# The second layer of a token-block MLP as seven half-size products instead of eight, on one Trainium2 core

## The chip, the cores and the metric

The kernel runs on one core of a Trainium2 (trn2) chip. A core has TensorE (PE in the profile; PEld is its weight load), VectorE (DVE), ScalarE (ACT), GpSimd (POOL) and SyncE (SP), and 16 DMA engines. The metric is the device time in microseconds (us). Kernels are compared by the runs of the same rounds: a ratio is worked out from these runs, and is not quite the ratio of the medians quoted beside it. TensorE was granted 0.994 to 1.0 of its clock. "Faster" needs 2%. The span in a profile (first to last instruction) is about 1.8 us shorter than the time.

## The reference, cut to what matters

Linear attention, then a gated MLP over 4608 tokens:

```python
# q, k, v: (8, 8, 576, 64); phi(x) = elu(x) + 1
kv  = einsum('bhsd,bhse->bhde', phi(k), v);  z = phi(k).sum(axis=2)
x   = einsum('bhsd,bhde->bhse', phi(q), kv) / (einsum('bhsd,bhd->bhs', phi(q), z) + 1e-6)
x   = x.transpose(...).reshape(4608, 512)
g   = x @ w_gate                               # 512 -> 1536
out = (g * sigmoid(g) * (x @ w_val)) @ w_out   # 1536 -> 512
```

The kernel works in f16 with f32 sums. It handles the MLP in nine groups of 512 tokens. In a group the **first layer** is 12 blocks (`fb`) of 8 matmuls of 512 columns, and the **second layer** multiplies the hidden block h (1536 x 512 tokens) by `w_out`. While a group runs, VectorE and ScalarE prepare the attention of later batches. `pV`, `pG` and `pX` are the eight banks of PSUM, the memory that TensorE writes its sums to; an *eviction* copies a bank to SBUF, the core's working memory.

## The kernel before

The second layer of one group takes four token tiles of 128, twelve matmuls of 512 columns each, and one eviction per tile:

```python
def l2(g, t, f0=0, f1=FB):                       # FB = 12
    pso[(g, t)] = (pV[0], pG[0], pV[1], pG[1])[t]
    for fb in range(f0, f1):
        nc.tensor.matmul(out=pso[(g, t)][:, :], lhsT=hT[g % 2][:, fb, P * t:P * t + P],
                         rhs=wo[:, fb, :], start=(fb == 0), stop=(fb == FB - 1))
```

The tile that ends the kernel is split into two halves of 256 columns (`l2_last`), so that its outputs can leave sooner. In the main loop, ahead of the fourth tile, two small pieces of TensorE work for later groups are made: `mm2` (the next group's x) and, right behind it, `joint` (k'v of the batch after):

```python
for t in range(4):
    if t == 3 and b1 < NG:
        mm2(b1, pV[2], "AVAV")      # next x: 16 small products for most groups, four evictions
        if b2 < B:
            joint(b2)               # next kv: small products, diagonals, R copies
    ...
    l2(g, t)
    for f in w[t] + pre[t]:         # exps and phi of later batches
        f()
    l2_out(g, t, A if t in (1, 3) else V)
```

`phi` of a batch costs VectorE a minimum and two `scalar_tensor_tensor` (max and add in one) per half:

```python
def phi(src, e, dst, b, lp):
    s = slice(2 * lp, 2 * lp + 2)
    nc.vector.tensor_scalar(out=e[:, s, :], in0=e[:, s, :], scalar1=1.0, scalar2=None, op0=ALU.min)
    for l in range(2 * lp, 2 * lp + 2):
        nc.vector.scalar_tensor_tensor(
            out=dst[b % 2][:, :, D * l:D * l + D],
            in0=src[b % 2][:, l, :].rearrange("p (j d) -> p j d", d=D), scalar=0.0,
            in1=e[:, l, :].rearrange("p (j d) -> p j d", d=D), op0=ALU.max, op1=ALU.add)
```

## Time and profile before

The time was 320.99 us (median of 3 runs, 320.7 to 321.11). The page's busy times, and its chain of the work that ended last, read:

```profile
span 319.2 us, 5573 instructions
...
PE 311.8 (98%) x2191; PEld 148.5 (47%) x2191; DVE 211.3 (66%) x393; ACT 171.3 (54%) x246; POOL 31.9 (10%) x47
...
PE 89%; DMA 4%; DVE 2%; POOL 2%; ACT 2%; issue 1%; SPq 0%; POOLq 0%; ACTq 0%
...
```

TensorE is busy for 98% and is 89% of the chain. Busy alone proves little, since the matmul ends are modelled; the starts say more. These are TensorE's lines of the timeline in one second layer and at the kernel's end (start, length, engine, line, operation, out<-in, shapes, count):

```profile
240.53 2.75 PE L303 MATMUL pV<-wo,hT 128*128 128x512 f16 x12
243.12 2.75 PE L303 MATMUL pG<-wo,hT 128*128 128x512 f16 x12
245.71 2.75 PE L303 MATMUL pV<-wo,hT 128*128 128x512 f16 x12
...
311.79 1.47 PE L324 MATMUL pG<-wo,hT 128*128 128x256 f16 x12
313.10 1.47 PE L324 MATMUL pX<-wo,hT 128*128 128x256 f16 x12
...
```

Twelve matmuls of 512 columns start 2.59 us apart, 0.216 us each; twelve of 256 columns 1.31 us apart, 0.109 us each. So matmuls of half the size cost half, although each has its own weight load. One whole group in the middle (window of group 4; columns: window, length, then busy us and instruction counts of each engine, clock, DMA share, GB/s):

```profile
154.35:186.96 32.61, 32.61 (x234) 15.21 (x233) 26.12 (x49) 19.55 (x29) 1.48 (x2) 1.00 0.56 105
```

A group takes 32.61 us: 20.94 for the first layer with one more product of 512 columns (the denominators of a later batch), and 11.67 for the second with `mm2` and `joint`. VectorE is busy for 26.1 us of it and ScalarE for 19.6.

At the end of the kernel, the last evictions and output DMAs follow the last matmul:

```profile
313.76 0.38 ACT L335 ACTIVATE osb<-pG 64x256 f32<-64x256 f32 x1 [3.75 <-DVE osb L332]
313.91 1.67 SPq L338 DMA_DIRECT2D out_dram<-osb  x2
...
314.67 0.42 DVE L332 TENSOR_SCALAR osb<-pX 64x256 f32<-64x256 f32 x1 [0.95 <-PE pX L324]
315.68 0.38 ACT L335 ACTIVATE osb<-pX 64x256 f32<-64x256 f32 x1 [1.55 <-DMA out_dram<-osb]
316.09 0.48 ACTq L338 DMA_DIRECT2D out_dram<-osb  x1
```

From the end of the last matmul (314.58) to the end of the span are 4.62 us. ScalarE's last eviction waits for a DMA that still reads its buffer.

### The profile page before, as it was taken

To read this page: it belongs to the slowest core of one execution; us is meant where nothing else is said; L and a number is where in the kernel's file an instruction comes from. 1 tells how busy PE (TensorE), PEld (TensorE's weight loads), DVE (VectorE), ACT (ScalarE), POOL (GpSimd) and SP (SyncE) were. 2 spreads that over 40 slices of the span, in tenths; PEclk is the share of its full clock that TensorE was granted. 3 is DMA by queue.
4 is the path that set the end of the run, shared out by engine and by line. 5 is a ranking of instruction groups with operands and counts; after the bars stand their busy time and mean duration, and the time that the engine had idled before them with its cause. 6 is when DMAs were issued, how large, how long until landed. Compare 5 with 4: busy or idle time off the path is not lost.

```text
span 319.2 us, 5573 instructions
## 1 busy us (share of the span) xinstructions
PE 311.8 (98%) x2191; PEld 148.5 (47%) x2191; DVE 211.3 (66%) x393; ACT 171.3 (54%) x246; POOL 31.9 (10%) x47
## 2 busy tenths in 40 slices
PE   8999999999999999999999999999999999999994
PEld 6644453444444454445444454445444444444443
DVE  3747749878978877887888787877883344134411
ACT  3869969748563765467536754585431333133310
POOL 8535310010020001000010000000000000000000
PEclk9999999999999999999999999999999999999999
DMA  7999999994579147924792430233022400140014
GB/s 101 194 200 200 204 207 208 260 210 85 118 140 166 33 93 139 154 46 90 142 149 50 87 74 0 49 71 89 2 49 59 101 0 0 35 99 0 2 35 97
DMA packets 40986, 32.21 MB, mean 101 GB/s; under 512 B 16256, under 2 KB 36480, under 8 KB 40960
## 3 DMA queue, kind: packets, MB, share of 16 engines
q0 software_dynamic: 20640, 18.88, 38.0%
q1 hardware_dynamic: 20160, 12.85, 18.4%
q8 instruction: 17, 0.28, 0.4%
q10 hardware_dynamic: 160, 0.13, 0.2%
q14 instruction: 9, 0.07, 0.1%
HBM read 37.75 MB, written 9.44 MB: 148 GB/s over the span
## 4 chain that ended last, share of the span: by engine, by line
PE 89%; DMA 4%; DVE 2%; POOL 2%; ACT 2%; issue 1%; SPq 0%; POOLq 0%; ACTq 0%
PE pV L282 28%; PE pG L282 27%; PE pV L303 14%; PE pG L303 13%; DMA wv<-in_moe_w_val_dram 3%; PE pX L282 2%; PE pX L254 1%; DVE osb L313 1%; DMA out_dram<-osb 1%; PE pV L172 1%; DVE xT L435 1%; ACT rr L432 1%; ACT rr L429 1%; POOL k L99 0%; POOL v L99 0%
## 5 line engine op out<-in xcount | busy, mean ns | idle before, releaser
L288 DVE SCALAR_TENSOR_TENSOR hT<-pV,sil 128x512 f16<-128x512 f32 x105 | 72.2, 691 | 57.0 <-PE pV L282 53.2
L282 PE MATMUL pV<-xT,wv 128*128 128x512 f16 x420 | 108.1, 379 | 0.3 <-DMA wv<-in_moe_w_val_dram 0.3
L282 PE MATMUL pG<-xT,wg 128*128 128x512 f16 x408 | 105.1, 379 | 0.7 <-DVE osb L313 0.6
L287 ACT ACTIVATE sil<-pG 128x512 f16<-128x512 f32 x102 | 60.6, 597 | 78.4 <-PE pG L282 51.2
L282 PEld LDWEIGHTS <-wv 128*128 128x128 f16 x432 | 42.2, 98 | 51.6 <-DMA wv<-in_moe_w_val_dram 1.1
L282 PEld LDWEIGHTS <-wg 128*128 128x128 f16 x432 | 41.8, 98 | 51.0 <-issue 1.5
L303 PEld LDWEIGHTS <-hT 128*128 128x128 f16 x420 | 39.8, 98 | 47.6 <-issue 1.2
L303 PE MATMUL pV<-wo,hT 128*128 128x512 f16 x216 | 50.2, 379 | 0.0
L303 PE MATMUL pG<-wo,hT 128*128 128x512 f16 x204 | 47.6, 380 | 0.0
L313 DVE TENSOR_SCALAR osb<-pV 128x512 f32<-128x512 f32 x18 | 12.4, 690 | 25.3 <-PE pV L303 25.3
L311 ACT ACTIVATE osb<-pG 128x512 f32<-128x512 f32 x15 | 8.8, 589 | 19.9 <-PE pG L303 19.8
L127 DVE SCALAR_TENSOR_TENSOR kp<-k,ek 128x576 f16<-128x576 f16 x24 | 17.1, 755 | 0.4
L127 DVE SCALAR_TENSOR_TENSOR qp<-q,eq 128x576 f16<-128x576 f16 x24 | 17.1, 755 | 0.4
L235 DVE TENSOR_TENSOR qp<-qp,rden 128x768 f16<-128x768 f16 x18 | 17.1, 949 | 0.0
L222 DVE TENSOR_REDUCE den<-prod 128x12 f32<-128x768 f16 x18 | 17.0, 943 | 0.0
L269 ACT ACTIVATE xT<-pX 128x512 f16<-128x512 f32 (+1 forms) x14 | 7.4, 579 | 16.7 <-PE pX L254 9.3
L121 ACT ACTIVATE ek<-k 128x1152 f16<-128x1152 f16 x14 | 15.6, 1154 | 0.1
L121 ACT ACTIVATE eq<-q 128x1152 f16<-128x1152 f16 x14 | 15.4, 1148 | 0.0
L147 ACT ACTIVATE vm<-v 128x1152 f16<-128x1152 f16 x12 | 14.1, 1175 | 0.0
L96 POOL DMA_DIRECT2D k<-in_k_dram x7 | 5.4, 766 | 76.8 <-DVE kp L127 53.8
L365 PE MATMUL pX<-sil,ones 128*128 128x256 f16 x51 | 8.9, 350 | 1.3 <-DVE sil L356 1.3
L217 DVE TENSOR_TENSOR prod<-qp,zbc 128x768 f16<-128x768 f16 x18 | 9.3, 516 | 1.4 <-ACT zbc L208 1.3
(105 smaller groups left out, 218.1 us busy)
## 6 DMA issues: line engine op xcount, KB each, us to landing
out_dram<-osb SPq DMA_DIRECT2D x70, 128.0 KB, 2.4
k<-in_k_dram POOLq DMA_DIRECT2D x7, 576.0 KB, 13.2
q<-in_q_dram POOLq DMA_DIRECT2D x7, 576.0 KB, 7.5
v<-in_v_dram POOLq DMA_DIRECT2D x7, 576.0 KB, 9.6
wg<-in_moe_w_gate_dram POOLq DMA_DIRECT2D x6, 256.0 KB, 11.7
wv<-in_moe_w_val_dram POOLq DMA_DIRECT2D x6, 256.0 KB, 11.9
wo<-in_moe_w_out_dram POOLq DMA_DIRECT2D x3, 512.0 KB, 15.8
k<-in_k_dram POOLq DMA_DIRECT2D x2, 288.0 KB, 5.7
```

Source lines behind the costliest of these rows:

```text
L121: nc.scalar.activation(out=e[:, s, :], in_=src[b % 2][:, s, :], func=AF.Exp, bias=0.0, scale=1.0)
L127: nc.vector.scalar_tensor_tensor(out=dst[b % 2][:, :, D * l:D * l + D], in0=src[b % 2][:, l, :].rearrange("p (j d) -> p j d", d=D), scalar ...
L147: nc.scalar.activation(out=vm[b % 2][:, :, s, 0:D].rearrange("p j l d -> p l j d"), in_=v16[b % 2][:, s, :].rearrange("p l (j d) -> p l j ...
L217: nc.vector.tensor_tensor(out=prod[:, 0:j1 - j0, :], in0=qp[b % 2][:, j0:j1, :], in1=zbc[:, :].unsqueeze(1).to_broadcast([P, j1 - j0, HL * ...
L222: nc.vector.tensor_reduce(out=den[:, HL * j0:HL * j1], in_=prod[:, 0:j1 - j0, :].rearrange("p j (l d) -> p (j l) d", d=D), axis=AX.X, op=A ...
L235: nc.vector.tensor_tensor(out=qv, in0=qv, in1=rden[:, HL * j0:HL * j1].unsqueeze(2).to_broadcast([P, HL * (j1 - j0), D]), op=ALU.mult)
L282: nc.tensor.matmul(out=ps[:, :], lhsT=src[:, i, P * fb:P * fb + P], rhs=xT[i][g % 2][:, :], start=(i == 0), stop=(i == 3))
L287: nc.scalar.activation(out=s[:, :], in_=pg[:, :], func=AF.Silu, bias=0.0, scale=1.0)
L288: nc.vector.scalar_tensor_tensor(out=hT[g % 2][:, fb, :], in0=pv[:, :], scalar=SC, in1=s[:, :], op0=ALU.mult, op1=ALU.mult)
L303: nc.tensor.matmul(out=pso[(g, t)][:, :], lhsT=hT[g % 2][:, fb, P * t:P * t + P], rhs=wo[:, fb, :], start=(fb == 0), stop=(fb == FB - 1))
L313: nc.vector.tensor_scalar(out=o[:, :], in0=ps[:, :], scalar1=1.0 / SC, scalar2=None, op0=ALU.mult)
L365: nc.tensor.matmul(out=dst[:, 0:256], lhsT=ones[:, :], rhs=sil[0][:, 0:256], start=True, stop=True)
```

## The change

The intent is to take TensorE work away. Strassen's scheme (in Winograd's form, with fifteen sums) multiplies two 2x2 block matrices with seven block products instead of eight. Groups 2 to 8 use it for the second layer: 7 products x 6 blocks x 2 token tiles = 84 matmuls of 256 columns in place of 48 of 512. Four sums of h (made on VectorE in thirds as h appears in the first layer), four sums of weights (made once), and three partial results per token tile, kept in SBUF, come with it. To pay for the sums on VectorE, the max of phi moves to ScalarE as a relu. A token tile of a product (`tt` in the diff) stands for a pair of tiles of 128 tokens, one in each half of the group. The last group runs one pair ahead of the other, so that outputs leave early.

```diff
+    def h_sum(g, m, f0, f1):                       # S1..S4, f16, a third of the blocks at a time
+        ...                                        # a, b, op: blocks of h or earlier sums, by m
+        nc.vector.tensor_tensor(out=hs[:, m, f0:f1, :], in0=a, in1=b, op=op)
+    def prd(g, n, tt):                             # product n of 7, token tile tt: six matmuls of 256 columns
+        for f in range(HF):
+            nc.tensor.matmul(out=(z if n in (2, 3, 5) else x)[:, 0:HD], lhsT=left(f), rhs=right(f), ...)
+    def keep(tt, i, from_x):  ...                  # ScalarE: partial result to SBUF, f32, 128x256
+    def fin(tt, th, ch, i, from_x):  ...           # VectorE: partial result + PSUM -> output block
+    def relu(src, dst, b, lp):  ...                # ScalarE: the max of phi
@@ main loop, g > 1
+                sl[3 + m].append(lambda m=m: h_sum(g, m, 0, 2))
+                sl[(8, 9, 9, 10)[m]].append(lambda m=m: h_sum(g, m, 2, 4))
+                sl[11].append(lambda m=m: h_sum(g, m, 4, 6))
+        for (i, step) in enumerate(l2_steps(g)):   # 14 products, with evictions and puts between them
+            ...
+            if i == 8 and b1 < NG:
+                mm2(b1, (pV[1], pG[1], pV[0], pG[0]), "AVAV")
+            if i == 10 and b2 < B:
+                joint(b2)
@@ the last group's order (k: keep, c: finish, d: put of half a row block)
+        return [(p[1][0],), (p[2][0], k1[0]), (p[6][0], c11[0], d[0][0][0]), (p[5][0], k2[0]), (p[1][1], k5[0]),
+                (p[7][0], k1[1]), (p[3][0], c22[0], d[0][1][1]), (p[2][1], c12[0], d[0][0][1]), (p[4][0], c11[1], d[1][0][0]),
+                (p[6][1], c21[0], d[0][1][0]), (p[5][1], k2[1]), (p[7][1], k5[1]), (p[3][1], c22[1], d22),
+                (p[4][1], c12[1], d12), (lambda: fin_last(g),)]
... (bank choices, weight sums on GpSimd in group 0 and VectorE in group 1, and prep slots cut)
```

More of the change, by code (lines that the diff above doesn't have):

```diff
@@ L74 @@
     osb = two([P, DM], FP32, "osb", 4)
+    hs = sb.tile([P, 4, FB // 2, U * C // 2], FP16, name="hs")
+    ws = sb.tile([P, 4, FB // 2, DM // 2], FP16, name="ws")
+    part = sb.tile([P, 6, DM // 2], FP32, name="part")
     wg = sb.tile([P, 4, DF], FP16, name="wg")
@@ L84 @@
     pX = [pp.tile([P, 512], FP32, name=f"pX_{i}") for i in range(3)]
-    turn = [0]
-    def bank():
-        turn[0] += 1
-        return pX[turn[0] % 3]
     def heads(src, b):
@@ L130, in phi, with relu, relu_k, relu_q @@
                 in1=e[:, l, :].rearrange("p (j d) -> p j d", d=D), op0=ALU.max, op1=ALU.add)
+    def relu(src, dst, b, lp):
+        s = slice(2 * lp, 2 * lp + 2)
+        nc.scalar.activation(out=dst[b % 2][:, :, P * lp:P * lp + P].rearrange("p j (s d) -> p s j d", d=D),
+                             in_=src[b % 2][:, s, :].rearrange("p s (j d) -> p s j d", d=D),
+                             func=AF.Relu, bias=0.0, scale=1.0)
+    def relu_k(b, lp):
+        relu(k16, kp, b, lp)
+    def relu_q(b, lp):
+        relu(q16, qp, b, lp)
+    def phi_sum(e, dst, b, lp):
+        s = slice(2 * lp, 2 * lp + 2)
+        nc.vector.tensor_scalar(out=e[:, s, :], in0=e[:, s, :], scalar1=1.0, scalar2=None, op0=ALU.min)
+        d = dst[b % 2][:, :, P * lp:P * lp + P].rearrange("p j (s d) -> p s j d", d=D)
+        nc.vector.tensor_tensor(out=d, in0=d, in1=e[:, s, :].rearrange("p s (j d) -> p s j d", d=D), op=ALU.add)
     def exp_k(b, lp):
@@ L138, in phi_k @@
     def phi_k(b, lp):
-        phi(k16, ek, kp, b, lp)
+        phi_sum(ek, kp, b, lp) if b > 2 else phi(k16, ek, kp, b, lp)
     def phi_q(b, lp):
-        phi(q16, eq, qp, b, lp)
+        phi_sum(eq, qp, b, lp) if b > 2 else phi(q16, eq, qp, b, lp)
     def vcast(b, lp):
@@ L159, in mm1 @@
         if lp == 0:
-            kvb[b] = ((pV[2], pX[0]), (pX[2], pV[2]), (pX[0], pX[1]), (pV[0], pG[0]))[min(b, 3)]
+            kvb[b] = ((pV[2], pX[0]), (pX[2], pV[2]), (pX[0], pX[1]), (pV[0], pG[0]), (pV[1], pG[1]))[min(b, 4)]
         for j in range(J):
@@ L200, in zb @@
     def zb(b):
-        zps[b] = bank()
+        zps[b] = pX[0]
         nc.tensor.matmul(out=zps[b][:, :], lhsT=ones[:, :], rhs=zd[:, :, :].rearrange("p i c -> p (i c)"),
@@ L255, in corners, with mm2 @@
                                      rhs=qT[b % 2][rows, j0:j1, lp, C * hh:C * hh + C], start=True, stop=True)
-    def mm2(g, spare, engs):
-        ps = [bank(), bank(), bank(), spare]
+    def mm2(g, ps, engs):
         us = units(g)
@@ L317, in l2_out @@
                               in_=o[C * e:C * e + C, :])
-    def l2_last(g, t):
-        banks = (pG[1], pX[0])
-        for h in range(2):
-            for fb in range(FB):
-                nc.tensor.matmul(out=banks[h][:, 0:256], lhsT=hT[g % 2][:, fb, P * t:P * t + P],
-                                 rhs=wo[:, fb, 256 * h:256 * h + 256], start=(fb == 0), stop=(fb == FB - 1))
-        for h in range(2):
-            for e in range(2):
-                o = osb[ot[0] % 4]
-                ot[0] += 1
-                rows = slice(C * e, C * e + C)
-                if e == 0:
-                    nc.vector.tensor_scalar(out=o[rows, 0:256], in0=banks[h][rows, 0:256], scalar1=1.0 / SC,
-                                            scalar2=None, op0=ALU.mult)
-                else:
-                    nc.scalar.activation(out=o[rows, 0:256], in_=banks[h][rows, 0:256], func=AF.Copy, bias=0.0,
-                                         scale=1.0 / SC)
-                b, j = units(g)[2 * t + e]
-                (nc.sync, nc.scalar)[e].dma_start(
-                    out=out[S * b:S * b + S, 256 * h:256 * h + 256].rearrange("(c j) f -> j c f", j=J)[j],
-                    in_=o[rows, 0:256])
@@ new lines, with h_blk, w_blk @@
+    HF, HT, HD = FB // 2, U * C // 2, DM // 2
+    def h_blk(g, kh, th, f0, f1):
+        return hT[g % 2][:, 2 * f0 + kh:2 * f1 - 1 + kh:2, HT * th:HT * th + HT]
+    def w_blk(kh, ch, f0, f1):
+        return wo[:, 2 * f0 + kh:2 * f1 - 1 + kh:2, HD * ch:HD * ch + HD]
+    def h_sum(g, m, f0, f1):
+        o = hs[:, m, f0:f1, :]
+        (a, b, op) = ((h_blk(g, 0, 1, f0, f1), h_blk(g, 1, 1, f0, f1), ALU.add),
+                      (hs[:, 0, f0:f1, :], h_blk(g, 0, 0, f0, f1), ALU.subtract),
+                      (h_blk(g, 0, 0, f0, f1), h_blk(g, 0, 1, f0, f1), ALU.subtract),
+                      (h_blk(g, 1, 0, f0, f1), hs[:, 1, f0:f1, :], ALU.subtract))[m]
+        nc.vector.tensor_tensor(out=o, in0=a, in1=b, op=op)
@@ new lines, in w_sum, with l2_banks, left, right @@
+    def w_sum(eng, m, f0, f1):
+        o = ws[:, m, f0:f1, :]
+        (a, b) = ((w_blk(0, 1, f0, f1), w_blk(0, 0, f0, f1)), (w_blk(1, 1, f0, f1), ws[:, 0, f0:f1, :]),
+                  (w_blk(1, 1, f0, f1), w_blk(0, 1, f0, f1)), (w_blk(1, 0, f0, f1), ws[:, 1, f0:f1, :]))[m]
+        eng.tensor_tensor(out=o, in0=a, in1=b, op=ALU.subtract)
+    def l2_banks(tt):
+        return (pX[0], pX[1])[tt], (pX[2], pV[2])[tt]
+    def prd(g, n, tt):
+        (x, z) = l2_banks(tt)
+        th = P * tt
+        def left(f):
+            h = hT[g % 2]
+            return {1: h[:, 2 * f, th:th + P], 2: h[:, 2 * f + 1, th:th + P], 3: hs[:, 3, f, th:th + P],
+                    4: h[:, 2 * f + 1, HT + th:HT + th + P], 5: hs[:, 0, f, th:th + P], 6: hs[:, 1, f, th:th + P],
+                    7: hs[:, 2, f, th:th + P]}[n]
+        def right(f):
+            return {1: wo[:, 2 * f, 0:HD], 2: wo[:, 2 * f + 1, 0:HD], 3: wo[:, 2 * f + 1, HD:DM], 4: ws[:, 3, f, :],
+                    5: ws[:, 0, f, :], 6: ws[:, 1, f, :], 7: ws[:, 2, f, :]}[n]
+        for f in range(HF):
+            nc.tensor.matmul(out=(z if n in (2, 3, 5) else x)[:, 0:HD], lhsT=left(f), rhs=right(f),
+                             start=(f == 0 and n in (1, 2, 5)), stop=(f == HF - 1), skip_group_check=True)
@@ new lines, in keep, with fin @@
+    def keep(tt, i, from_x):
+        (x, z) = l2_banks(tt)
+        nc.scalar.activation(out=part[:, 2 * i + tt, :], in_=(x if from_x else z)[:, 0:HD], func=AF.Copy, bias=0.0,
+                             scale=1.0 / SC)
+    def fin(tt, th, ch, i, from_x):
+        (x, z) = l2_banks(tt)
+        nc.vector.scalar_tensor_tensor(out=osb[2 * th + tt][:, HD * ch:HD * ch + HD],
+                                       in0=(x if from_x else z)[:, 0:HD], scalar=1.0 / SC, in1=part[:, 2 * i + tt, :],
+                                       op0=ALU.mult, op1=ALU.add)
@@ new lines, in put, with fin_21, fin_last @@
+    def put(g, tt, th, c0=0, c1=DM, engs=(nc.sync, nc.sync)):
+        for e in range(2):
+            b, j = units(g)[2 * (2 * th + tt) + e]
+            engs[e].dma_start(out=out[S * b:S * b + S, c0:c1].rearrange("(c j) f -> j c f", j=J)[j],
+                              in_=osb[2 * th + tt][C * e:C * e + C, c0:c1])
+    def fin_21(g, tt):
+        x = l2_banks(tt)[0]
+        nc.scalar.activation(out=osb[2 + tt][:, 0:HD], in_=x[:, 0:HD], func=AF.Copy, bias=0.0, scale=1.0 / SC)
+    def fin_last(g):
+        x, o = l2_banks(1)[0], osb[3]
+        nc.vector.tensor_scalar(out=o[0:C, 0:HD], in0=x[0:C, 0:HD], scalar1=1.0 / SC, scalar2=None, op0=ALU.mult)
+        nc.scalar.activation(out=o[C:P, 0:HD], in_=x[C:P, 0:HD], func=AF.Copy, bias=0.0, scale=1.0 / SC)
+        put(g, 1, 1, 0, HD, (nc.sync, nc.scalar))
@@ new lines, in l2_steps @@
+    def l2_steps(g):
+        p = [[(lambda n=n, tt=tt: prd(g, n, tt)) for tt in range(2)] for n in range(8)]
+        k1, k2, k5 = [[(lambda i=i, tt=tt, x=x: keep(tt, i, x)) for tt in range(2)]
+                      for (i, x) in ((0, True), (1, True), (2, False))]
+        c11 = [lambda tt=tt: fin(tt, 0, 0, 0, False) for tt in range(2)]
+        c22 = [lambda tt=tt: fin(tt, 1, 1, 2, True) for tt in range(2)]
+        c12 = [lambda tt=tt: fin(tt, 0, 1, 1, False) for tt in range(2)]
+        c21 = [lambda tt=tt: fin_21(g, tt) for tt in range(2)]
+        o1, o2 = [[(lambda tt=tt, th=th: put(g, tt, th)) for tt in range(2)] for th in range(2)]
+        if g < NG - 1:
+            return [(p[1][0],), (p[1][1], k1[0]), (p[2][0], k1[1]), (p[2][1], c11[0]), (p[6][0], c11[1]),
+                    (p[6][1], k2[0]), (p[5][0], k2[1]), (p[5][1], k5[0]), (p[7][0], k5[1]), (p[7][1], c22[0]),
+                    (p[3][0], c22[1]), (p[3][1], c12[0], o1[0]), (p[4][0], c12[1], o1[1]), (p[4][1], c21[0], o2[0]),
+                    (c21[1], o2[1])]
+        d = [[[(lambda tt=tt, th=th, ch=ch: put(g, tt, th, HD * ch, HD * ch + HD)) for ch in range(2)]
+              for th in range(2)] for tt in range(2)]
+        d22 = lambda: put(g, 1, 1, HD, DM, (nc.sync, nc.scalar))
+        d12 = lambda: put(g, 1, 0, HD, DM, (nc.sync, nc.gpsimd))
+        return [(p[1][0],), (p[2][0], k1[0]), (p[6][0], c11[0], d[0][0][0]), (p[5][0], k2[0]), (p[1][1], k5[0]),
+                (p[7][0], k1[1]), (p[3][0], c22[0], d[0][1][1]), (p[2][1], c12[0], d[0][0][1]), (p[4][0], c11[1], d[1][0][0]),
+                (p[6][1], c21[0], d[0][1][0]), (p[5][1], k2[1]), (p[7][1], k5[1]), (p[3][1], c22[1], d22),
+                (p[4][1], c12[1], d12), (lambda: fin_last(g),)]
@@ L585, in steady @@
     def steady(b):
-        n = 5 if b == 2 else 2
+        n = 5 if b == 2 else 2 if b == 3 else 1
         items = [(n, lambda: zb(b)), (n, lambda: zb_copy(b)), (n, lambda: s3_prod(b, 0)),
@@ L596, in steady @@
                      (2, lambda: phi_q(2, 1)), (3, lambda: joint(2))] + items
-        else:
+        elif b == 3:
             items = [(0, lambda: phi_q(b, 1))] + items
@@ L601, in prep @@
     def prep(b):
-        return at(4, [(0, lambda: exp_k(b, 0)), (0, lambda: exp_k(b, 1)), (1, lambda: exp_q(b, 0)),
-                      (1, lambda: exp_q(b, 1)), (1, lambda: phi_k(b, 0)), (2, lambda: phi_k(b, 1)),
-                      (3, lambda: nc.scalar.preload_act_table_set("silu_and_others")), (3, lambda: phi_q(b, 0))])
+        (k0, k1, q0, q1, p0, p1, tb, r0, r1) = (2, 6, 8, 9, 5, 7, 14, 13, 14) if b > 3 else (0, 0, 1, 1, 1, 2, 3, 3, 3)
+        return at(16, [(k0, lambda: exp_k(b, 0)), (k1, lambda: exp_k(b, 1)), (q0, lambda: exp_q(b, 0)),
+                       (q1, lambda: exp_q(b, 1)), (p0, lambda: phi_k(b, 0)), (p1, lambda: phi_k(b, 1)),
+                       (tb, lambda: nc.scalar.preload_act_table_set("silu_and_others")), (r0, lambda: phi_q(b, 0))]
+                  + ([(r1, lambda: phi_q(b, 1))] if b > 3 else []))
     def ld_b(b):
@@ L646 @@
     for i in range(3):
+        if i < 2:
+            for m in range(4):
+                w_sum(nc.gpsimd, m, 2 * i, 2 * i + 2)
         for t in range(4):
@@ L657 @@
         sl, w = [[] for _ in range(FB)], [[] for _ in range(4)]
-        pre = [[] for _ in range(4)]
+        pre = [[] for _ in range(16)]
         if b1 < B:
@@ L662 @@
             pre = prep(b2)
-            sl[8].append(lambda: vcast(b2, 0))
-            sl[9].append(lambda: vcast(b2, 1))
+            for lp in range(2):
+                sl[4 + lp].append(lambda lp=lp: relu_k(b2, lp))
+                sl[6 + lp].append(lambda lp=lp: relu_q(b2, lp))
+                sl[8 + lp].append(lambda lp=lp: vcast(b2, lp))
+        for m in range(4):
+            if g == 1:
+                sl[3 + m].append(lambda m=m: w_sum(nc.vector, m, 4, 6))
+            else:
+                sl[3 + m].append(lambda m=m: h_sum(g, m, 0, 2))
+                sl[(8, 9, 9, 10)[m]].append(lambda m=m: h_sum(g, m, 2, 4))
+                sl[11].append(lambda m=m: h_sum(g, m, 4, 6))
         for fb in range(FB):
@@ L672 @@
                 ld_b(3)
-        for t in range(4):
-            if t == 3 and b1 < NG:
-                mm2(b1, pV[2], "AVAV")
-                if b2 < B:
+        if g == 1:
+            for t in range(4):
+                if t == 3:
+                    mm2(b1, (pX[0], pX[1], pX[2], pV[2]), "AVAV")
                     joint(b2)
-            if g == NG - 1 and t == 3:
-                l2_last(g, t)
-                continue
-            l2(g, t)
-            for f in w[t] + pre[t]:
-                f()
-            l2_out(g, t, A if t in (1, 3) else V)
+                l2(g, t)
+                for f in w[t] + pre[t]:
+                    f()
+                l2_out(g, t, A if t in (1, 3) else V)
+            continue
+        for (i, step) in enumerate(l2_steps(g)):
+            for f in step:
+                f()
+            if i == 8 and b1 < NG:
+                mm2(b1, (pV[1], pG[1], pV[0], pG[0]), "AVAV")
+            for f in pre[i]:
+                f()
+            if i == 10 and b2 < B:
+                joint(b2)
 _INS = ['q', 'k', 'v', 'moe_w_gate', 'moe_w_val', 'moe_w_out']
```

## The prediction

> **What bounds the kernel now.** TensorE. The page shows PE busy 311.8 of 319.2 us (98%), granted clock 0.998, and the chain of waits is 89% PE. In the timeline one group's first layer (96 matmuls of 512 columns) takes 20.7 us and its second (48) 4 x 2.59 = 10.36 us, 0.216 us per matmul, with almost no PE wait. Groups 2 to 5 take about 32.6 us each: 31.1 us of layers, the rest small products for the next batch. DVE is busy about 26 us and ACT about 19.5 us of that.
>
> **What the change removes.** In groups 2 to 8 the 48 products of 512 columns become 84 of 256. The old last token tile already runs 24 products of 256 columns: 1.31 us per 12, so 0.109 us each, weight loads hidden. (The Trainium skill, "TensorE: Matmul & The Clock Gate", back-to-back issue gap, gives N/2.4 + 2.5 ns: 109 and 216; the trace agrees.) So 84 x 0.109 = 9.17 against 10.36: 1.19 us per group, 8.3 us in seven, all on the critical path.
>
> **What it adds, off the path.** DVE: twelve half-width sums of h per group, about 0.38 us each (estimate from the 128x768 f16 product at 0.516), 4.4 us, and six 256-wide finishes of about 0.42 in place of two 0.69 evictions. It loses 3 us per prepared batch, because the max of phi goes to ACT (two 755 ns operations become one f16 add of 758). ACT gains four relus of about 1.17 us and six keeps of about 0.38. My slot count: a first-layer slot is 1.73 us of PE; DVE is asked for 1.75 to 1.85 in most late slots, 1.48 in one, less early; the backlog at the layer's end is about 0.3 us, and three pV banks absorb it. ACT's slots with a relu or cast are 1.73 too. So both are nearly saturated in the first layer, without a PE stall there. The sums in thirds leave four for the end of the layer: done 2.5 us into the second layer; the first product that needs them starts at 2.6 us.
>
> **What is given back.** (a) Groups 2 to 5: the joint products for the next batch follow the xT evictions by only about 1.3 us, behind two exps, two phi sums and a table load: 0.3 us of stall a group, about 1 us. (b) The last group runs one token pair ahead: its fourth product needs the bank that DVE frees only after all four late sums: 0.6 us. (c) GpSimd makes two thirds of the weight sums during group 0; the skill ("SBUF — State Buffer", who interferes with whom) says that two-input DVE operations block with GpSimd reads; no run shows the size here; 0.3 us. (d) The tail shrinks by about 1 us: today ScalarE's last eviction waits 1.55 us for an output DMA that holds its buffer; the new one has its own.
>
> **Sum.** 8.3 + 1.0 - 1.0 - 0.6 - 0.3 = 7.4 us: 320.99 becomes about 313.5 us (2.3%), range 311.3 to 316.6. Faster by over 2% (below 314.6): 0.70; within 2%: 0.28; slower: 0.02.
>
> **What would show it.** Right: second layers of 9.2 us plus the small products; groups 2 to 5 near 31.6 us; PE above 96%; DVE near 28 us a group; the last PE work to the end of the span under 4 us. Wrong: PE waits on DVE sums (hs), ACT keeps or xT; h sums at 0.6 us (half rate); matmuls of 256 columns above 0.115 us.
>
> **What would make it wrong.** DVE's FIFO: sums slower than 0.45 us would delay hT and stall PE in every group; ACT's backlog at the second layer's start; a slower group 0.

## The result, and the profile after

The changed kernel took 314.95 us (median of 4 runs, 314.63 to 315.06) against 320.85 us in the same rounds (320.45 to 321.11). The ratio is 0.9819, with an interval of 0.9805 to 0.9833: 1.8% faster, which at the 2% mark counts as the same. The time lies in the predicted range, 1.4 us above the predicted value.

```profile
span 313.1 us, 6257 instructions
...
PE 303.5 (97%) x2431; PEld 170.7 (55%) x2431; DVE 232.0 (74%) x488; ACT 203.6 (65%) x307; POOL 41.3 (13%) x56
...
SPq 1%; DMA 1%; PE 0%; ACT 0%; issue 0%; DVE 0%
...
```

TensorE is still 97% busy. The chain that ended last now begins in the output queue (SPq is SyncE's issuing of DMAs) and is not followed far back, so it says something of the end only. Group 4 after:

```profile
152.47:184.05 31.58, 31.58 (x271) 18.57 (x269) 28.17 (x60) 25.26 (x38) 0.86 (x2) 1.00 0.48 96
```

The group is 1.03 us shorter. VectorE is busy for 28.2 of 31.6 us (the prediction said near 28), and ScalarE went from 19.6 to 25.3. The h sums took 0.418 us each (predicted 0.38).

The starts in the timeline give every group's length. The second layer is taken from its first product to the first product of the next group, and in group 8 to the end of the last matmul:

| us | before | after | saved |
|---|---|---|---|
| start of group 1 | 55.58 | 55.47 | 0.11 |
| group 1 | 33.56 | 33.82 | -0.26 |
| groups 2 to 5, each | 32.60 to 32.63 | 31.59 | 1.01 to 1.04 |
| groups 6 and 7 | 31.97, 31.74 | 30.78, 30.55 | 1.19 each |
| group 8 | 31.27 | 31.10 | 0.17 |
| last matmul to the end | 4.62 | 4.98 | -0.36 |

The sum, 0.11 - 0.26 + 4.10 + 2.38 + 0.17 - 0.36 = 6.14 us, is the difference of the spans but for rounding (319.20 - 313.05 = 6.15). Groups 6 and 7 give just the 1.19 us that the count of matmuls promised. Groups 2 to 5 give 0.17 us less each, group 8 gives 1.02 us less, and the end takes longer instead of shorter. What happens in group 8 and after it is in these lines of the timeline (bracketed: how long the engine sat idle, and who released it):

```profile
299.00 1.02 PE L373 MATMUL pX<-ws,hs 128*128 128x256 f16 x6
299.15 0.42 DVE L347 TENSOR_TENSOR hs<-hs,hT 128x512 f16<-128x512 f16 x1
299.49 0.42 DVE L347 TENSOR_TENSOR hs<-hT 128x512 f16<-128x512 f16 x1
...
299.82 0.42 DVE L347 TENSOR_TENSOR hs<-hT,hs 128x512 f16<-128x512 f16 x1
...
300.16 0.42 DVE L383 SCALAR_TENSOR_TENSOR osb<-pX,part 128x256 f32<-128x256 f32 x1
300.60 10.06 SPq L390 DMA_DIRECT2D out_dram<-osb  x13
300.63 0.81 PE L373 MATMUL pX<-ws,hs 128*128 128x256 f16 x6 [0.61 <-DVE osb L383]
...
308.11 0.42 DVE L399 TENSOR_SCALAR osb<-pX 64x256 f32<-64x256 f32 x1 [0.31 <-PE pX L373]
308.56 0.38 ACT L400 ACTIVATE osb<-pX 64x256 f32<-64x256 f32 x1 [2.11 <-DMA out_dram<-osb]
308.97 0.48 ACTq L390 DMA_DIRECT2D out_dram<-osb  x1
```

The third product (299.00) takes 1.02 us instead of 0.82, as it waits for a sum of h. The fourth starts at 300.63, 1.63 us after the third where 0.66 is the pace: 0.97 us lost, since VectorE makes the finish that frees the bank (300.16) only after all four late sums. At the end, the last evictions are done by 308.94, but SyncE's 13 output DMAs keep its queue until 300.60 + 10.06 = 310.66. ScalarE's last eviction starts as VectorE's ends (308.53): both read one bank, and the kernel's semaphores make the one wait for the other. The bracket names a DMA that landed at about the same moment; it was issued at 306.66 and reads another of the four output buffers.

### The profile page after: what moved, and what is told of

Its sections match the earlier page's. It is cut to its first block, busy times and chain, and to the rows that moved or that the text cites. A ratio compares the mean times of both kernels' runs of the same rounds, so it can differ in the third digit from the quotient of the medians.

```text
span 313.1 us, 6257 instructions
## 1 busy us (share of the span) xinstructions
PE 303.5 (97%) x2431; PEld 170.7 (55%) x2431; DVE 232.0 (74%) x488; ACT 203.6 (65%) x307; POOL 41.3 (13%) x56
## 5 line engine op out<-in xcount | busy, mean ns | idle before, releaser
L373 PEld LDWEIGHTS <-hs 128*128 128x128 f16 x336 | 32.0, 98 | 5.9 <-issue 1.6
L373 PE MATMUL pX<-ws,hs 128*128 128x256 f16 x210 | 26.9, 273 | 0.6 <-DVE osb L383 0.6
L373 PEld LDWEIGHTS <-hT 128*128 128x128 f16 x252 | 24.6, 98 | 4.4
L378 ACT ACTIVATE part<-pX 128x256 f32<-128x256 f32 x35 | 12.9, 382 | 15.0 <-PE pX L373 15.0
L347 DVE TENSOR_TENSOR hs<-hT 128x512 f16<-128x512 f16 x42 | 17.5, 417 | 0.3
L373 PE MATMUL pX<-wo,hT 128*128 128x256 f16 x126 | 15.1, 273 | 0.0
L383 DVE SCALAR_TENSOR_TENSOR osb<-pX,part 128x256 f32<-128x256 f32 x28 | 11.0, 416 | 4.6 <-PE pX L373 2.4
L317 PEld LDWEIGHTS <-hT 128*128 128x128 f16 x96 | 8.6, 98 | 10.2 <-issue 0.8
L285 DVE TENSOR_SCALAR xT<-pG 128x512 f16<-128x512 f32 x12 | 7.7, 683 | 6.5 <-PE pG L269 6.5
```

The source lines that it names most:

```text
L347: nc.vector.tensor_tensor(out=o, in0=a, in1=b, op=op)
L373: nc.tensor.matmul(out=(z if n in (2, 3, 5) else x)[:, 0:HD], lhsT=left(f), rhs=right(f), start=(f == 0 and n in (1, 2, 5)), stop=(f == HF ...
L378: nc.scalar.activation(out=part[:, 2 * i + tt, :], in_=(x if from_x else z)[:, 0:HD], func=AF.Copy, bias=0.0, scale=1.0 / SC)
L383: nc.vector.scalar_tensor_tensor(out=osb[2 * th + tt][:, HD * ch:HD * ch + HD], in0=(x if from_x else z)[:, 0:HD], scalar=1.0 / SC, in1=pa ...
```

## The experiments

Two theories of the lost 1.4 us stood at the start. **A**: the repeated part is as predicted, and the loss is in the last group and behind it, in VectorE's order and SyncE's queue. **B**: VectorE and ScalarE, nearly full, hold TensorE back in every group. Four runs (e1 to e4) shared their rounds (before: 320.73 us), the next four (a1, a2, a3, a5) too (320.7), and then after_again, a4 and best (320.74). best2 ran a little later. This table has what all their traces show of the second layers (start to start) and of the end:

| us | time | groups 2 to 5 | groups 6, 7 | group 8 | last matmul to the end |
|---|---|---|---|---|---|
| after | 314.95 | 10.65 | 9.84 | 10.38 | 4.98 |
| after_again | 314.78 | 10.65 | 9.84 | 10.38 | 4.68 |
| e1_rows | 313.98 | 10.65 | 9.84 | 10.38 | 4.29 |
| e2_one_evict | 315.09 | 10.65 | 9.84 | 10.38 | 5.38 |
| e3_order8 | 313.66 | 10.65 | 9.84 | 9.41 | 4.70 |
| e4_joint11 | 314.48 | 10.65 | 9.84 | 10.38 | 4.69 |
| a1_phi_on_dve | 318.07 | 11.48 | 9.84 | 10.38 | 4.69 |
| a2_sums_at_end | 325.44 | 12.53, then 11.79 | 10.98 | 12.52 | 4.67 |
| a3_last_as_others | 315.18 | 10.65 | 9.84 | 9.33 | 6.57 |
| a4_no_h_sums | 313.44 | 10.65 | 9.84 | 9.49 | 4.67 |
| a5_split_mm2 | 315.95 | 10.88 | 10.07 | 10.38 | 4.69 |
| best | 313.88 | 10.65 | 9.84 | 9.41 | 4.82 |
| best2 | 312.84 | 10.65 | 9.84 | 9.41 | 3.94 |

The start of group 0 varies between traces from 15.9 to 17.0 us, so spans of single traces differ by as much without meaning anything.

### Control: the changed kernel again

> The changed kernel once more, as the control of these rounds: 314.9 us, within 0.4.

It took 314.78 us, ratio 0.9816 (0.9802 to 0.9829), as expected.

### Do the sums on VectorE slow TensorE? (a4_no_h_sums)

```diff
-                sl[3 + m].append(lambda m=m: h_sum(g, m, 0, 2))
-                ... (the other two thirds)
+                if g == 2:                      # made once, stale afterwards: wrong results on purpose
+                    sl[3 + m].append(lambda m=m: h_sum(g, m, 0, 2))
+                    ...
```

> The changed kernel with the sums of h made in group 2 alone and left standing for the later groups (wrong results on purpose, the same products and evictions). Theory (in thirds they are free, save in the last group): groups 3 to 7 stay at 31.59 and 30.77 within 0.05 us, the last second layer falls from 10.38 to 9.4, 0.8 to 1.1 us in all. Rival (the sums on VectorE slow every group): 3 us or more.

313.44 us, 1.3 us under the control. Groups 3 to 7 did not change by a hundredth of a microsecond in the table; group 8 fell from 10.38 to 9.49. So the 5.0 us of sums per group (12 x 0.418) are free everywhere but in the last group. Theory B falls for the sums.

### Do they stay free elsewhere? (a2_sums_at_end)

```diff
-                sl[3 + m].append(lambda m=m: h_sum(g, m, 0, 2))
-                sl[(8, 9, 9, 10)[m]].append(lambda m=m: h_sum(g, m, 2, 4))
-                sl[11].append(lambda m=m: h_sum(g, m, 4, 6))
+                sl[11].append(lambda m=m: h_sum(g, m, 0, 6))
```

> The changed kernel with each sum of h made once, at the end of the first layer, instead of in thirds inside it. Theory: four operations of about 0.9 us follow the last hT; the first finish on VectorE comes at about 4.9 us of the second layer instead of 3.0, so the product that needs its bank waits about 1 us in groups 2 to 7 and about 2 us in group 8: the second layers become 11.6 us and 10.8 us, the time 320 to 323 us, the whole gain gone. Rival (the sums hide wherever they stand): within 1 us of the changed kernel.

325.44 us (324.0 to 325.84), 1.4% slower than the kernel before. TensorE now waits in all seven groups:

```profile
PE pX L373 <- DVE osb L383: 4.7, 7, 1.2
PE pX L373 <- DVE hs L347: 3.6, 7, 1.5
...
```

(The columns of the waits: who waited for whom, us in total, times, longest.) The first line is the wait for the finish behind the sums, the second for the sums themselves. The second layers grew by 1.14 us in groups 3 to 7, 1.88 in group 2 and 2.14 in group 8. The time is a miss upwards: 320 to 323 us were expected. The five runs also differ by more than is usual here, from 324.0 us (the traced one, span 322.2) to 325.84; the three slowest are those with the lowest granted clock (0.994 to 0.995, against 0.998 and 1.0). Whether that is the cause is open; the fastest is slower than every run of the kernel before.

### Does VectorE need the room that the relus bought? (a1_phi_on_dve)

```diff
     def phi_k(b, lp):
-        phi_sum(ek, kp, b, lp) if b > 2 else phi(k16, ek, kp, b, lp)
+        phi(k16, ek, kp, b, lp)
     ... (phi_q likewise; the four relu slots taken out)
```

> The changed kernel with the max of phi back on VectorE (ScalarE's four relus a batch taken out). Theory (VectorE is nearly full, 28 of 31.6 us a group, so its room had to be bought by moving the max): VectorE gets about 2.7 us more per prepared batch, the xT evictions and the joint products wait about 1 us, and the backlog runs into the next first layer; groups 2 to 5 grow from 31.59 to 32.5 or more, the time to 317 to 320 us. Rival (TensorE's count alone decides, VectorE has slack): groups 2 to 5 stay within 0.2 us of 31.59.

318.07 us. Groups 2 to 5 took 32.42 us each, 0.83 more, and TensorE waits where expected:

```profile
PE pG L187 <- DVE xT L285: 2.5, 4, 0.6
```

That is the first product of `joint`, waiting for an eviction of x that VectorE makes late. The backlog did not run on into the next first layer (20.94 us, unchanged). So over half of the gain depends on moving work from VectorE to ScalarE. Group 1 was 33.56 us here, as before the change, and 33.71 in the control: the relus cost 0.15 us there.

### Is the 0.2 us in groups 2 to 5 a wait for the evictions of x? (e4_joint11, a5_split_mm2)

The list of waits of the changed kernel has this line, and the prediction's term (a) says the same:

```profile
PEld L187 <- DVE xT L285: 0.8, 4, 0.2
```

```diff
-            if i == 10 and b2 < B:
+            if i == 11 and b2 < B:
                 joint(b2)
```

> The joint products for the next batch one product later (after the twelfth of fourteen). Theory: the second layers of groups 2 to 5 go from 10.65 to about 10.45 us, the waits of the weight loads of kp on xT (0.8 us in total) vanish, 0.4 to 0.8 us in all. Rival: what follows the joint products (diagonals, R copies, the next layer's first gate) is late instead and the gain is under 0.2 us.

`joint` stood one product (0.66 us) later and the second layers stayed at 10.65 us to the hundredth; the same line with the same 0.8 us stood in the list of waits. So it was no wait for data. (The time, 314.48 us, ratio 0.9806 with an interval of 0.9791 to 0.9821, overlaps the control's; its trace shows no shorter stretch of TensorE.) The other explanation is that TensorE loses time when it changes between 128x128 and 64x64 products. The Trainium skill, "TensorEngine Tiling (Array Packing)", Key Properties, says that a change of tiling mode drains TensorE, without a figure. Before the change `joint` followed `mm2` at once, with one change there and one back for both; after it, two products lie between, so there are two of each. The next run adds one more pair of changes:

```diff
-            if i == 8 and b1 < NG:
-                mm2(b1, (pV[1], pG[1], pV[0], pG[0]), "AVAV")
+            if i in (7, 8) and b1 < NG:                      # half of the heads each time
+                mm2(b1, (pV[1], pG[1], pV[0], pG[0]), "AVAV", (i - 7,))
```

> The small products of the next x in two halves with one half-size product between them. Theory (each change between 128x128 and 64x64 products costs TensorE about 0.1 us, which is what the joint products, now apart from the x products, cost in groups 2 to 5): one more change there and back, 0.17 to 0.25 us in each of groups 2 to 7, second layers of 10.85 and 10.05 us, 1.0 to 1.5 us in all. Rival (the 0.2 us are a wait for the evictions of xT): no change or slightly faster, within 0.3 us.

315.95 us, and 10.88 and 10.07 us in the table: 0.23 us more in every one of the six groups, with the same products and evictions. A change there and back, with the split that makes it, costs 0.23 us; the theory of waits is out. The starts in the trace of the changed kernel show the same at each change:

```profile
178.64 0.82 PE L373 MATMUL pX<-ws,hs 128*128 128x256 f16 x6
179.39 0.32 PE L269 MATMUL pV<-qT,R 64*64 64x320 f16 x1
...
179.78 0.24 PE L269 MATMUL pG<-qT,R 64*64 64x192 f16 x1
179.95 0.83 PE L373 MATMUL pX<-ws,hs 128*128 128x256 f16 x6
180.62 0.82 PE L373 MATMUL pX<-wo,hs 128*128 128x256 f16 x6
181.37 0.22 PE L187 MATMUL pV<-vm,kp 64*64 64x65 f16 x2
...
```

Six matmuls of 256 columns take 0.66 us, but the first small product starts 0.75 us after them, before x (178.64 to 179.39) as before `joint` (180.62 to 181.37), and in e4 too, one product later (180.66 to 181.41): 0.09 us for the change there. The change back shows after the last small product of x: 0.17 us to the next start (179.78 to 179.95), where the kernel before went on to `joint` after 0.08 (183.54 to 183.62 in its trace). Together that is the 0.17 us of groups 2 to 5, within the rounding. That the cause is a drain is the skill's statement; the runs show only what the change costs.

### The last group's order (e3_order8)

```diff
-                sl[11].append(lambda m=m: h_sum(g, m, 4, 6))
+                if g < NG - 1 or m < 2:
+                    sl[11].append(lambda m=m: h_sum(g, m, 4, 6))
...
-        return [(p[1][0],), (p[2][0], k1[0]), (p[6][0], c11[0], ...), (p[5][0], k2[0]), (p[1][1], k5[0]), ...
+        return [(p[1][0],), (p[2][0], k1[0]), (p[1][1], c11[0], *late, ...), (p[6][0], k1[1]), (p[5][0], k2[0]),
+                (p[2][1], k5[0]), (p[7][0], c11[1], ...), (p[6][1], c22[0], ...), (p[3][0], k2[1]), ...   # late: the two other sums
```

> Last group: the first product of the second token pair moved before the product that needs the late sums, and the finish that frees the bank queued on VectorE ahead of two of the four late sums. Theory: the 0.61 us wait of TensorE for that finish and the 0.2 us for the sums vanish, the last matmul ends about 0.8 us earlier; the time falls by 0.6 to 0.9 us only if SyncE's queue, which then starts its issues earlier, moves too; if the queue holds the end regardless, by under 0.5.

313.66 us, 1.1 to 1.3 us under the two measurements of the changed kernel. The last second layer fell from 10.38 to 9.41 us, the full pace; the end came earlier by as much, as SyncE's queue started earlier too.

### What holds the end (e1_rows, e2_one_evict, a3_last_as_others)

e1_rows puts whole rows of 512 columns where half rows were put, so that SyncE issues 7 DMAs instead of 13:

```diff
     ... (the first puts, d[0][0][0], go likewise)
-                (p[7][0], k1[1]), (p[3][0], c22[0], d[0][1][1]), (p[2][1], c12[0], d[0][0][1]), (p[4][0], c11[1], d[1][0][0]),
-                (p[6][1], c21[0], d[0][1][0]), ...
+                (p[7][0], k1[1]), (p[3][0], c22[0]), (p[2][1], c12[0], o1[0]), (p[4][0], c11[1]),
+                (p[6][1], c21[0], o2[0]), ...
```

> Theory (SyncE's issue queue sets the end): the last group issues 13 output DMAs on SyncE's queue at about 0.64 us each; the last issue is at 310.12 us, 1.6 us after its data were ready, and lands last at 312.12. With whole rows put where two halves of a row were put before, SyncE issues 7 and is free in time: the last landing becomes ScalarE's at about 311.1, so the span shrinks by 0.7 to 1.1 us, from 313.05 to about 312.1. Rival (the serial last evictions, VectorE then ScalarE, set the end): no change, within 0.2 us.

313.98 us, 0.8 to 1.0 under the changed kernel, and 4.29 us from the last matmul to the end. These lines answer to those of the changed kernel's end:

```profile
303.50 5.12 SPq L390 DMA_DIRECT2D out_dram<-osb  x7
...
308.16 0.38 ACT L400 ACTIVATE osb<-pX 64x256 f32<-64x256 f32 x1 [2.11 <-DVE osb L399]
308.57 0.48 ACTq L390 DMA_DIRECT2D out_dram<-osb  x1
```

SyncE is done at 308.62, before ScalarE's last issue ends (309.05); in the changed kernel it was done at 310.66, 1.2 us after it (309.45). The line of ScalarE shows its true releaser now, VectorE. e2_one_evict makes that last eviction in one VectorE operation of 128 partitions:

```diff
-        nc.vector.tensor_scalar(out=o[0:C, 0:HD], in0=x[0:C, 0:HD], ...)
-        nc.scalar.activation(out=o[C:P, 0:HD], in_=x[C:P, 0:HD], ...)
+        nc.vector.tensor_scalar(out=o[:, 0:HD], in0=x[:, 0:HD], ...)
```

> One VectorE eviction of 128 partitions in place of VectorE's and ScalarE's of 64 each, which run one after the other. Theory (SyncE's queue sets the end): within 0.2 us of the changed kernel, 314.95 us, since the landing at 312.12 comes from SyncE's queue. Rival (the serial evictions set the end): 0.4 us faster.

315.09 us: nothing, as the theory of the queue has it. (Its end of 5.38 us is one trace's: the last issue was done 2.58 us after the last matmul, as in the changed kernel with 2.59, and only the landing took longer.) a3_last_as_others takes the stagger out:

```diff
-        if g < NG - 1:
+        if True:                      # the last group too: the order of the others, whole rows put
             return [(p[1][0],), (p[1][1], k1[0]), (p[2][0], k1[1]), (p[2][1], c11[0]), ...
```

> The last group in the order of the other groups, whole rows put, no stagger of the token pairs. Theory: the stagger costs 1.0 us of TensorE waits and 13 issues of 0.64 us; without it the last second layer takes about 9.35 us instead of 10.38 and the eight late puts on SyncE's queue then set the end, about 4.8 us after the last matmul: 0.7 to 1.2 us faster in all, about 314. Rival (the stagger pays, since outputs leave earlier): 1 us or more slower.

A miss: 315.18 us, no gain. TensorE was 1.05 us faster in group 8, but the end took 6.57 us. All outputs come late in this order. So the stagger as written gave back in TensorE waits what it won in early outputs.

### Together (best, best2)

> The changed kernel with whole rows put, one last eviction, and the last group's new order together. Theory: the last second layer takes 9.4 us instead of 10.38, and the stretch from the last matmul to the end 4.1 instead of 4.7 to 5.0 us: 1.5 to 1.9 us faster than the changed kernel, 313.0 to 313.4 us, 2.3 to 2.45% under the kernel before.

`best` joins e1, e2 and e3. A miss again: 313.88 us, 0.9791 (0.9778 to 0.9805), no better than e1 or e3 alone. TensorE did what was expected (9.41), but the end took 4.82 us. In single microseconds of the windows, the DMA engines' share and GB/s are the last two columns (first `after`, then `best`; the last matmul ends at 308.07 and at 307.30):

```profile
307.00:308.00 1.00, 1.00 (x10) 0.64 (x7) 0.63 (x2) 0.00 (x0) 0.00 (x0) 1.00 0.37 85
308.00:309.00 1.00, 0.07 (x1) 0.00 (x0) 0.42 (x1) 0.38 (x1) 0.56 (x1) 1.00 0.69 159
...
```

```profile
307.00:308.00 1.00, 0.30 (x3) 0.01 (x1) 0.45 (x2) 0.00 (x0) 0.56 (x1) 1.00 0.98 211
308.00:309.00 1.00, 0.00 (x0) 0.00 (x0) 0.00 (x0) 0.00 (x0) 0.00 (x0) 1.00 0.84 203
...
```

In the changed kernel the DMA engines are well short of full while SyncE issues. In `best` the first outputs of the group are issued at 304.4, more than 6 us into its second layer, and from 306 to 310 the DMA engines are nearly full at about 205 GB/s (201 to 211 in three of those microseconds, 256 in one): the group's 1.05 MB of output needs 5.1 us at that rate. The remedy is half rows, so that outputs start early, with their issues shared by two queues:

```diff
-        d = [[[(lambda ...: put(g, tt, th, HD * ch, HD * ch + HD)) ...
+        d = [[[(lambda ...: put(g, tt, th, HD * ch, HD * ch + HD, (nc.sync, nc.gpsimd))) ...
```

(with the order of e3 and the single eviction of e2)

> The new order of the last group and the single last eviction, with the half rows kept (so that outputs start about 4 us earlier than in the run of whole rows) but their issues shared between SyncE's and GpSimd's queues. Theory (in the run of whole rows the DMA engines were 0.84 to 0.98 busy from one microsecond before the last matmul to the end, about 205 GB/s, and in the changed kernel SyncE's issues fed them at half of that): neither the issue queue nor the transfers hold the end now; the last matmul is followed by about 3.6 to 4.2 us instead of 4.7, the time is 312.7 to 313.4 us. Rival (the transfers bind whatever the order): as the run of whole rows, 313.9 us within 0.3.

312.84 us (median of 6 runs, 312.59 to 313.12), ratio 0.9754 (0.9742 to 0.9766): faster than the kernel before by 2.5% and than the control by 1.9 us, with correct results. From e3 it differs by the single eviction, which gained nothing in e2, and by the shared issues: 0.8 us in time, and 3.94 against 4.70 us at the end. The end:

```profile
300.17 8.12 SPq L390 DMA_DIRECT2D out_dram<-osb  x8
...
306.50 1.83 ACTq L390 DMA_DIRECT2D out_dram<-osb  x2
...
307.36 0.53 POOL L390 DMA_DIRECT2D out_dram<-osb  x1 [0.83 <-DVE osb L383]
307.38 0.42 DVE L399 TENSOR_SCALAR osb<-pX 128x256 f32<-128x256 f32 x1 [0.31 <-PE pX L373]
```

All three queues are done by 308.4, about 1 us after the last matmul, and 3.94 us in all follow it.

## Why the prediction was right or wrong

The time lay in the range and the main mechanism held, but the prediction put 0.70 on "faster by over 2%", and 1.8% came. Term by term:

- **"84 x 0.109 = 9.17 against 10.36: 1.19 us per group, 8.3 us in seven, all on the critical path."** Right: 1.19 us in groups 6 and 7, which have nothing else in the way.
- **The sums are made "without a PE stall there" (first layer).** Right: the first layers stayed at 20.94 us, and without the sums (a4) the groups are as long. It holds only for this placement: with the sums at the end (a2) the gain is more than lost, and without the relus (a1) over half of it is.
- **(a) "0.3 us of stall a group, about 1 us", for xT evictions.** The size is near (0.17 us in four groups, 0.7 in all), by luck, for the mechanism was wrong: e4 moved the products out of the way of the evictions and nothing changed, and a5 and the starts showed what does cost, about 0.2 us for each extra change to 64x64 products and back.
- **(b) "its fourth product needs the bank that DVE frees only after all four late sums: 0.6 us".** Right in mechanism, shown by e3; the size was 0.97 us, with 0.2 of it a wait for the sums themselves.
- **(c) "GpSimd makes two thirds of the weight sums during group 0 ... 0.3 us."** Not seen: from its first matmul to the start of group 1, group 0 takes 38.98 us before, and 38.8 to 39.6 in the thirteen traces with these sums (middle value 39.0). The Trainium skill, "SBUF — State Buffer", who interferes with whom, speaks of VectorE operations with two inputs in SBUF; in the trace VectorE runs none of those while GpSimd's eight sums (1.16 us each, 38.8 to 48.9) run, only operations with at most one input in SBUF. So this doesn't test it. What did cost was ScalarE in group 1, by 0.15 us (a1 against the control).
- **(d) "The tail shrinks by about 1 us ... the new one has its own."** (The tail is the stretch from the last matmul to the end; "its own" is a buffer.) This is the step that failed, and the largest: 4.98 and 4.68 us were measured against 4.62, so 1.1 to 1.4 us are missing where 5.9 us came for 7.4 (the other terms nearly cancel, which is luck: (a) and (c) came out 0.7 better than forecast, (b) 0.4 worse, and group 1 lost 0.1 to 0.3 that nobody forecast). The wait for the buffer did go, as forecast. But the change also raised the output DMAs of the last group from 10 to 16, those on SyncE's queue from 8 to 13, at 0.55 us of issue and about 0.64 us from start to start each, and the prediction counted matmuls and evictions, not issues. e1 showed it by taking issues away (4.29 us), best2 by sharing them (3.94), e2 by shortening the evictions without effect. The forecast was about 3.6; what keeps best2 above it isn't shown.

## What to carry to other kernels

Where TensorE is the bound, seven products for eight do pay what the count says, provided that the added sums are made in pieces while their inputs appear, and that the vector engine's new work is paid for by moving other work off it. Count the instructions of every queue in the last few microseconds, DMA issues included, since two limits, the issues and the transfers, lie close together there and removing one shows the next (shortening the eviction gained nothing): the fixes of the order and of the issues were worth about 1 us each, no more than 1 us together in `best`, and 1.9 us only when the transfers started early as well. A wait of TensorE beside a change of product size is not always a wait for data; move the product before you believe it.

## What the Trainium skill lacked or had wrong

- "TensorE: Matmul & The Clock Gate", Back-to-back issue gap: it gives about 131 ns per matmul of 512 columns for a real stream of weight loads and matmuls, and calls N/2.4 + 2.5 ns an isolated gap. Here such streams run at 216 ns (512 columns, 12 in 2.59 us) and 109 ns (256 columns, 12 in 1.31 us), each matmul with its own weight load: the formula holds, the 131 ns does not.
- "TensorEngine Tiling (Array Packing)", Key Properties: it says that a change of tiling mode drains TensorE, without a cost. Here a change to 64x64 products and back costs about 0.2 us (a5: 10.65 to 10.88, 9.84 to 10.07; 0.17 in groups 2 to 5).
- "DMA: Bandwidth & Descriptors", Issuing engines are not separate DMA queues: it says that issuing from several engines only saves the sequencer's time, usually small beside the DMA itself. For outputs of 64 KB it is not small: about 0.64 us from issue to issue on SyncE's queue feeds about 100 GB/s (an estimate from 65.5 KB an issue; 83 to 114 were moved from 305 to 309 us in after_again), where the transfers reached 205 GB/s (`best`), and sharing the issues was worth 0.8 us (e3 to `best2`).
- No page gives for this chip the rate at which one core's outputs, in rows of 1 to 2 KB, leave for HBM; here about 205 GB/s with the DMA engines 0.84 to 0.98 busy.
